# A fused attention and gMLP kernel: VectorE's exp as a squared square with a linear part summed by TensorE, denser Q projections, one accumulation for two output products, other head and tail

## The chip, the cores and the metric

The kernel runs on one core of one Trainium2 chip. The metric is the device time of one execution in microseconds (us), the median of several runs. Before the change it is 902.68 us, the median of 3 runs (899.88 to 902.83). The runs of the kernel before agree within a few tenths of a per cent; those of the kernels after the change scatter more, by about 1%. (A run is rated slow here when it is over 1.5% above the fastest run of its kernel.)

The engines are named as in the profile: PE is TensorE (matmuls), PEld its weight loads, ACT is ScalarE, DVE is VectorE, POOL is GpSimd, SP is the engine that issues most transfers.

## The reference

```python
# x: (1, 2048, 512); 32 heads of 16; one K and one V head for all (MQA); FH = 688
g = sigmoid((x * gate_w).sum(-1, keepdims=True))

q = (x @ wq).reshape(B, S, 32, 16).transpose(0, 2, 1, 3)
k, v = x @ wk, x @ wv
p = softmax(einsum("bhqd,bkd->bhqk", q, k) * 16 ** -0.5)
a = einsum("bhqk,bkd->bhqd", p, v).transpose(0, 2, 1, 3).reshape(B, S, 512) @ wo

z = gelu(x @ w_in)                       # (2048, 1376), tanh form
z1, z2 = z[..., :688], layernorm(z[..., 688:])
b = (z1 * (w_sp @ z2 + b_sp[:, None])) @ w_out

out = g * a + (1 - g) * b
```

The dominant work is the softmax: 32 x 2048 x 2048 exponentials. The product with `w_sp` (2048 x 2048, called the spatial matmuls below) is the largest dense product.

## The kernel before

The scores of four heads and 512 queries are made in blocks of 128 keys by 512 queries, 2048 blocks in all. A score matmul uses a 32-row tile of the array (a head has 16 rows, padded to 32), and up to four run together: in the trace of this kernel their starts lie 3 to 4 ns apart. The product with V (PV) uses a 32-column tile, again up to four together:

```python
def s_mm(dst_bank, blk, key):
    u, kt, g = blk
    mm(bank(dst_bank), KA[32*g:32*g+32, 128*kt:128*kt+128], QA[32*g:32*g+32, u % 4, :], True, True,
       [("K", kt // 4), ("Q", u % 4)], [key], tp=(32 * g, 0), chan="s", tag="S")     # 32 rows x 128 columns

def pv_mm(blk, src, key):
    ...
    mm(ps[32*g:32*g+32, 512*BO:512*BO+512], V1[:, kt, :], src, n == 0, n == NKT - 1,
       [("V", kt // 4), key], [("bk", BO)], tp=(0, 32 * g), chan="p", tag="PV")       # 128 rows x 32 columns
```

Most blocks get their exp on ACT, two or three blocks in one instruction from two alternating groups of PSUM banks. The others go to DVE in batches of four: one eviction per block, then nine operations over the batch (range reduction and a cubic polynomial):

```python
def d_A(m, i):
    op("dve", lambda v: v.tensor_scalar(DX[:, m % 2, 512*i:512*i+512], bank(BD), C_LOG2, 100.0, ALU.mult, ALU.min), ...)

def d_poly(m):
    return [
        (C4, ts(DN[:], x, BIG, BIG, ALU.add, ALU.subtract, ...)),
        (C2, tt(x, x, DN[:], ALU.subtract, ...)),
        (C4, ts(DT[:], x, E2[3], E2[2], ALU.mult, ALU.add, ...)),
        (C4, ts(n_i, DN[:], -126.0, 128.0, ALU.max, ALU.mult, ...)),
        (C2, tt(DT[:], DT[:], x, ALU.mult, ...)),
        (C4, ts(DT[:], DT[:], E2[1], None, ALU.add, ALU.bypass, ...)),
        (C2, tt(DT[:], DT[:], x, ALU.mult, ...)),
        (C4, ts(t_b, DT[:], E2[0], None, ALU.add, ALU.bypass, ...)),
        (C2, tt(pd.bitcast(I16), t_i, n_i, ALU.add, ...)),
    ]
```

All order is fixed when the program is built, by a small list scheduler in the source (`pe_pick`, `act_pick`, `dve_pick`). It plays the three engines forward with rough durations. Scores for ACT have the highest priority on PE. Everything that uses the whole array (projections, spatial matmuls, the products with `w_out` and `wo`) is cut into groups that share one PSUM bank, BM, and is slipped in where PE is free, one matmul at a time:

```python
elif misc["cur"].pos < len(misc["cur"].pieces):
    g = misc["cur"]                       # the group that owns bank BM

    def emit5():
        g.pieces[g.pos][1]()              # one full-array matmul
        g.pos += 1
    ...
    cands.append((now, 3, g.pieces[g.pos][0], emit5, fin5))
```

A group's bank comes free when DVE has evicted it, so each group ends with a wait for DVE. How many blocks go to DVE is decided by the same scheduler, as DVE has time (`new_batch`): 65 batches, 260 blocks; 1788 blocks are left for ACT in 715 instructions.

## Time and profile before

| | before |
|---|---|
| median time | 902.68 us |
| span of the profiled run | 897.0 us |
| ACT busy / DVE busy / PE busy | 94% / 94% / 89% |
| exp instructions on ACT | 715, 821.9 us |
| first exp starts, last exp ends | 12.6 us, 874.3 us |
| ACT idle between them | 16.8 us |
| mean granted TensorE clock | 0.978 |

First lines of the profile page of the kernel before: busy time of each engine, and busy tenths in 40 equal slices of the span (9 is 90% or more). PEclk is the granted TensorE clock in tenths of full speed.

```profile
PE 796.6 (89%) x5013; PEld 232.2 (26%) x5097; DVE 844.5 (94%) x1270; ACT 846.2 (94%) x729; POOL 7.0 (1%) x12
PE   5899989899995389999999999999999999999983
DVE  3299999999999999999999999999999999999995
ACT  4999999999999989999999999999999999999990
PEclk9999999999998599999999999999999999999998
```

ACT and DVE are both full from about 45 us to the end: the kernel is balanced between them. The clock row has one dip, in the stretch in which ACT does the gelu and PE has little to do (the clock is 0.50 from 284 to 315 us).

Costliest groups of instructions of the kernel before: line, engine, operation, output and input, shapes, count; busy us and mean ns of one; idle us of the engine just before them and what ended most of it.

```profile
L452 ACT ACTIVATE P<-ps 128x1536 bf16<-128x1536 f32 x715 | 821.9, 1258 | 24.6 <-PE ps L280 20.0
L280 PE MATMUL ps<-QA,KA 32*128 32x512 bf16 x2048 | 351.8, 387 | 52.5 <-DVE DX L466 28.0
L466 DVE TENSOR_SCALAR DX<-ps 128x512 f16<-128x512 f32 x260 | 177.3, 682 | 2.7 <-PE ps L280 2.4
L481 DVE TENSOR_TENSOR DT<-DT,DX 128x2048 f16<-128x2048 f16 x130 | 158.5, 1219 | 1.7
```

The exp costs 821.9/715 = 1.15 us of ACT each. A DVE operation over a batch costs 1.22 us as TENSOR_TENSOR and 0.685 us as TENSOR_SCALAR. DVE waited for nothing (2.7 us in all before its 260 evictions).

The windows view of the kernel before: from and to in us, length, then busy us and number of instructions of PE, PEld, DVE, ACT and POOL, the mean granted clock, the DMA share and GB/s.

```profile
core 0: us, PE busy (x) PEld busy (x) DVE busy (x) ACT busy (x) POOL busy (x), PEclk, DMA share, GB/s
740.00:840.00 100.00, 94.38 (x597) 27.46 (x605) 98.64 (x142) 98.88 (x87) 0.00 (x0) 1.00 0.00 1
...
783.00:809.00 26.00, 24.70 (x157) 7.31 (x159) 25.57 (x37) 25.78 (x24) 0.00 (x0) 1.00 0.00 1
```

The timeline of PE in the kernel before (start, length, what; matmuls of one kind that follow each other in one row):

```profile
785.80 0.38 PE L279 MATMUL ps<-wT,z 128*128 128x512 bf16 x1
786.11 0.39 PE L280 MATMUL ps<-QA,KA 32*128 32x512 bf16 x3
786.43 0.40 PE L280 MATMUL ps<-P,V 128*32 128x512 bf16 x3
...
788.48 0.39 PE L280 MATMUL ps<-QA,KA 32*128 32x512 bf16 x3
788.80 0.40 PE L280 MATMUL ps<-P,V 128*32 128x512 bf16 x3
```

A full matmul, three scores and three PVs follow each other at 0.32 us (786.11 to 786.43). The recorded lengths (0.38 to 0.40 us) are longer than that, so the matmuls overlap in the record; I go by the distance of the starts.

### The profile page before, as it was taken

What the parts mean: (1) busy time and instruction counts of PE and PEld (TensorE: products, weight loads), DVE (VectorE), ACT (ScalarE), POOL (GpSimd) and SP (SyncE); (2) the same over time, 40 slices, a digit from 0 to 9 for tenths busy, and PEclk for the clock granted to TensorE, in tenths of its full rate; (3) what the DMA queues carried; (4) which work ended last, traced back from release to release, by engine and by line L of the source; (5) the groups of instructions that cost most, each with busy time, mean ns of one, the idle gap of its engine ahead of it and who ended that gap; (6) DMA issues with size and microseconds to landing.
All of it is one profiled execution on the core that took longest, in us unless ns stands there. A gap on an engine that the chain in (4) does not pass through costs nothing.

```text
span 897.0 us, 13120 instructions
## 1 busy us (share of the span) xinstructions
PE 796.6 (89%) x5013; PEld 232.2 (26%) x5097; DVE 844.5 (94%) x1270; ACT 846.2 (94%) x729; POOL 7.0 (1%) x12
## 2 busy tenths in 40 slices
PE   5899989899995389999999999999999999999983
PEld 1323222222221022222222222222222222222220
DVE  3299999999999999999999999999999999999995
ACT  4999999999999989999999999999999999999990
POOL 1000000000000100000000000000000000000000
PEclk9999999999998599999999999999999999999998
DMA  6430000000000000001200003100002200000001
GB/s 131 130 72 1 1 1 1 1 1 1 1 1 1 0 1 1 1 1 33 63 1 1 1 1 60 35 1 1 1 1 48 48 1 1 1 1 1 17 31 49
DMA packets 48500, 16.66 MB, mean 19 GB/s; under 512 B 44161, under 2 KB 47921, under 8 KB 48434
## 3 DMA queue, kind: packets, MB, share of 16 engines
q1 hardware_dynamic: 45794, 15.23, 7.3%
q10 hardware_dynamic: 2640, 0.56, 0.4%
q8 instruction: 41, 0.67, 0.3%
q14 instruction: 25, 0.20, 0.1%
HBM read 3.20 MB, written 2.10 MB: 6 GB/s over the span
## 4 chain that ended last, share of the span: by engine, by line
DVE 69%; PE 18%; issue 8%; ACT 4%; DMA 1%; ACTq 0%; DVEq 0%
DVE DX L466 13%; DVE DT L481 13%; PE ps L280 12%; DVE DT L478 10%; DVE PD L481 7%; DVE DN L478 6%; DVE DX L481 6%; PE ps L279 6%; ACT P L452 3%; DVE bst L369 2%; DVE T L500 2%; DVE QA L324 2%; DVE z L348 1%; DVE z L355 1%; DVE z L402 1%
## 5 line engine op out<-in xcount | busy, mean ns | idle before, releaser
L452 ACT ACTIVATE P<-ps 128x1536 bf16<-128x1536 f32 x715 | 821.9, 1258 | 24.6 <-PE ps L280 20.0
L280 PE MATMUL ps<-QA,KA 32*128 32x512 bf16 x2048 | 351.8, 387 | 52.5 <-DVE DX L466 28.0
L280 PE MATMUL ps<-P,V 128*32 128x512 bf16 x1788 | 281.6, 392 | 1.9 <-DVE T L500 0.9
L466 DVE TENSOR_SCALAR DX<-ps 128x512 f16<-128x512 f32 x260 | 177.3, 682 | 2.7 <-PE ps L280 2.4
L280 PEld LDWEIGHTS ps<-QA,KA 32*128 32x128 bf16 x2048 | 85.6, 91 | 291.0 <-ACT P L452 141.6
L481 DVE TENSOR_TENSOR DT<-DT,DX 128x2048 f16<-128x2048 f16 x130 | 158.5, 1219 | 1.7
L280 PEld LDWEIGHTS ps<-P,V 128*32 128x32 bf16 x1788 | 68.2, 93 | 167.7 <-issue 158.9
L279 PE MATMUL ps<-wT,z 128*128 128x512 bf16 x349 | 108.2, 386 | 2.6 <-issue 2.2
L478 DVE TENSOR_SCALAR DT<-DT 128x2048 f16<-128x2048 f16 (+1 forms) x130 | 89.4, 688 | 2.4
L481 DVE TENSOR_TENSOR PD<-DT,DN 128x2048 int16<-128x2048 int16 x65 | 79.5, 1223 | 1.8
L481 DVE TENSOR_TENSOR DX<-DX,DN 128x2048 f16<-128x2048 f16 x65 | 79.4, 1221 | 1.5
L478 DVE TENSOR_SCALAR DT<-DX 128x2048 f16<-128x2048 f16 x65 | 44.5, 684 | 0.4
L478 DVE TENSOR_SCALAR DN<-DX 128x2048 f16<-128x2048 f16 x65 | 44.5, 684 | 0.3
L478 DVE TENSOR_SCALAR DN<-DN 128x2048 int16<-128x2048 f16 x65 | 44.5, 685 | 0.0
L279 PEld LDWEIGHTS ps<-wT,z 128*128 128x128 bf16 x384 | 28.9, 97 | 54.4 <-issue 45.5
L279 PE MATMUL ps<-xT,wq_pad 128*128 128x512 bf16 x111 | 36.3, 393 | 5.1 <-DVE z L348 1.8
L280 PE MATMUL ps<-PD,V 128*32 128x512 bf16 x260 | 31.9, 388 | 8.6 <-DVE PD L481 7.2
L279 PE MATMUL ps<-win,xT 128*128 128x344 bf16 x128 | 31.2, 315 | 1.3 <-DVE z L355 0.7
L279 PE MATMUL ps<-wout,z 128*128 128x512 bf16 x88 | 28.0, 385 | 2.3 <-DVE ybG L416 1.0
L279 PE MATMUL ps<-xT,win 128*128 128x512 bf16 x86 | 27.9, 385 | 2.2 <-DVE z L348 1.6
L279 PE MATMUL ps<-wo,OT 128*128 128x512 bf16 x59 | 18.9, 392 | 8.8 <-DVE outsb L432 3.7
L324 DVE CAST QA<-ps 128x512 bf16<-128x512 f32 x32 | 21.6, 676 | 2.7 <-PE ps L279 2.6
(66 smaller groups left out, 278.4 us busy)
## 6 DMA issues: line engine op xcount, KB each, us to landing
out_dram<-outsb SPq DMA_DIRECT2D x16, 128.0 KB, 1.7
win<-in_B_w_in_dram SPq DMA_DIRECT2D x1, 1376.0 KB, 6.5
wout<-in_B_w_out_dram SPq DMA_DIRECT2D x1, 640.0 KB, 4.4
wo<-in_A_wo_dram SPq DMA_DIRECT2D x8, 64.0 KB, 2.3
ybG<-in_A_wq_dram ACTq DMA_DIRECT2D x1, 448.0 KB, 4.7
wT<-in_B_w_sp_dram SPq DMA_TRANSPOSE x16, 4.4
xT<-in_A_x_dram SPq DMA_TRANSPOSE x4, 4.6
ybG<-in_A_wq_dram ACTq DMA_DIRECT2D x1, 64.0 KB, 3.8
```

The costliest lines, as they stand in the source:

```text
L279: return t.matmul(dst, lhsT, rhs, start=start, stop=stop)
L280: return t.matmul(dst, lhsT, rhs, start=start, stop=stop, tile_position=tp)
L324: ev = lambda: op("dve", lambda v: v.tensor_copy(QA[:, u % 4, :], bank(BM)), r=[BMK], w=[("Q", u % 4)], tag="Qev")
L348: ev = lambda: op("dve", lambda v: v.tensor_copy(z1[:, ft, 512 * tc:512 * tc + 512], bank(BM)), r=[BMK], w=[("z1", ft)], tag="z1ev")
L355: ev = lambda: op("dve", lambda v: v.tensor_copy(z2[:, FH * st + 344 * h:FH * st + 344 * h + 344], bank(BM, 344)), r=[BMK], w=[("z2", st)] ...
L369: dve_q.append((440, lambda st=st, h=h: op("dve", lambda v: v.bn_stats(bst[:, st, h, :], z2[:, FH * st + 344 * h:FH * st + 344 * h + 344]) ...
L402: ev = lambda: op("dve", lambda v: v.tensor_tensor(dst, ps[0:n, 512 * BM:512 * BM + 512], dst, ALU.mult), r=[BMK, ("z1", ft)], w=[("u", ft ...
L452: op("act", lambda a: a.activation(P[:, k % NP, 0:512 * n], ps[:, 512 * b0:512 * (b0 + n)], ACT.Exp), r=[("sc", k % 2)], w=[("P", k % NP)] ...
L466: op("dve", lambda v: v.tensor_scalar(DX[:, m % 2, 512 * i:512 * i + 512], bank(BD), C_LOG2, 100.0, ALU.mult, ALU.min), r=[("bk", BD)], w= ...
L478: return lambda: op("dve", lambda v: v.tensor_scalar(o, i, a, b, f, g), r=r, w=w, tag="dT")
L481: return lambda: op("dve", lambda v: v.tensor_tensor(o, i, j, f), r=r, w=w, tag="dTT")
L500: res = [(660, lambda: o("dve", lambda v: v.transpose(T1[:], bank(BO)), r=[("bk", BO)], w=["T1"], tag="T1"), setT(("O", u)))]
```

## The change

The intent is to make DVE's exp cheaper so that DVE can take blocks from ACT, and to shorten the head and the tail.

1. **Exp on DVE.** exp(x) is approximated by (u^2 + c)^2 with u linear in x, plus a linear function of x. The squared square takes three operations over a batch instead of nine. The linear part needs no elementwise work: summed over keys against V it is a product of Q with a small matrix (K^T V, precomputed), so TensorE adds it to the PV accumulation by two extra 32-column matmuls per head group ("corrections", 256 in all).
2. **Dense Q.** Q is projected for 128 columns at a time instead of 64 padded ones, so half the Q matmuls and evictions go. A copy of K shifted by 16 rows serves the odd heads.
3. **yb and wo in one PSUM group.** The products with `w_out` and `wo` accumulate in one bank, with the gate ratio folded into the softmax's normalisation, so the intermediate `ybG` and its eviction go.
4. **Head and tail.** Warm-up matmuls at the start, other order of transfers and projections; the last four output tiles are accumulated in free banks before the last exp.

The core of the diff (cuts marked by `...`):

```diff
         def d_A(m, i):
-            op("dve", lambda v: v.tensor_scalar(DX[:, m % 2, 512*i:512*i+512], bank(BD), C_LOG2, 100.0, ALU.mult, ALU.min), ...)
+            op("dve", lambda v: v.tensor_scalar(X[:, m % NX, 512*i:512*i+512], bank(BD), PA, PB, ALU.mult, ALU.add), ...)
         def d_poly(m):
-            return [ ... nine operations ... ]
+            return [
+                (C2, lambda: op("dve", lambda v: v.tensor_tensor(x, x, x, ALU.mult), ...)),
+                (C4, lambda: op("dve", lambda v: v.tensor_scalar(x, x, PC, None, ALU.add), ...)),
+                (C2, lambda: op("dve", lambda v: v.tensor_tensor(PD[:, m % ND, :], x, x, ALU.mult), ...)),
+            ]
+        def cor_mm(u, g, z):
+            n = (64 - units[u]["hi"]) // 4
+            if z == 0:
+                pv_raw(u, g, MC[:, n-1, 2*g + u % 2, :], QA[:, (u // 2) % NQ, :], ["MC", ("Q", (u // 2) % NQ)], "COR")
+            else:
+                pv_raw(u, g, CC[:, n-1, :], ones[:], ["CC", "ones"], "COR")
...
-        def g_yb(t2): ...
-        def g_wo(t2): ...
+        def g_fin(t2):
+            ...
+            return Group("fin", [(C512, lambda ft=ft: yb_mm(t2, ft, BM)) for ft in range(6)] +
+                                [(C512, lambda jp=jp: wo_mm(t2, jp, BM)) for jp in range(4)], [(680, ev)], ...)
...
-        first = deque([g_K(0), g_Q(0), g_V(0), g_K(1), g_V(1), g_K(2), g_V(2), g_K(3), g_V(3), g_Q(1)])
+        first = deque([g_V(0), g_K(1), g_K(2), g_V(1), g_K(3), g_V(2), g_V(3), g_MC(), g_R(0), g_Q(1), g_R(1), g_R(2), g_R(3)])
```

## The prediction

> **What bounds it now.** The table of engine busy time gives ACT 846 and DVE 845 of 897 us. By windows, 440 to 840 us has both 98 to 99% busy: balanced. PE shows 95% there, but the timeline says that is not its peak: a stream of full matmuls advances every 0.216 us, and each change between full, row-tiled (scores) and column-tiled (PV) matmuls advances 0.32 us, about 0.107 us for the change. [...] The first exp starts at 12.6 us (the first matmuls advance only every 0.43 us), and the last ends at 874.3, leaving a tail of 22.7 us: serial wo groups and DVE evictions.

> **Changes, costed** (counts from the built program):
> - VectorE exp: nine ops of 128x2048 per batch of four blocks (five TENSOR_SCALAR at 0.685, four TENSOR_TENSOR at 1.22) become three (two at 1.22, one at 0.685). With four evictions at 0.68 a batch falls from 11.0 to 5.85 us. [...]
> - The schedule takes only 89 batches, up from 65. Blocks on ACT fall from 1788 to 1692, ACT exps from 715 to 677. At 821.9/715 = 1.15 us each that is -44 us of ACT.
> - DVE: 89x5.85 = 521 instead of 717 for exp; the rest about 180 instead of 197 (16 fewer Q evictions at 0.68, no ybG at 0.74; new squares). Less the records' overlap, about 645 us busy, 77%: DVE becomes slack.
> - PE: 64 Q matmuls fewer, 256 correction matmuls (64 waves) more. In the built order waves (matmuls on different tiles, run together) fall from 2585 to 2472, mode changes from 2086 to 1946: at 0.216 and 0.107 us, 782 to 742 us. Not the bound.
> - Head: warm-up matmuls, Q projected without waiting for K's eviction and evicted by ACT: first exp about 9.5 us, -3.
> - Tail: yb and wo of the last four tiles are accumulated beforehand in free banks; after the last exp remain PV, transposes, four matmuls, evictions on two engines, output: about 12 us, -10.

> **Critical path.** ACT alone then sets the pace. Sum: 9.5 + 677x1.15 + about 26 (gelu, table loads, small) + about 15 idle (now 17) + 12.5 = 841 us of span; the runs are 5.7 us over the span: **about 846 us**, 80% range **830 to 862**, that is -6%. Of the gain of 57, 44 is ACT blocks moved; most of DVE's saving (200 us) is not spent.

> Chances: faster 0.95, same 0.04, slower 0.01.

> **What would show it.** Right: ACT 97% or more of the time from first to last exp, about 805 us busy; DVE 74 to 80%; squared-square ops at 1.22 and 0.69; first exp near 9.5; tail 11 to 14 us. Wrong: ACT idle grown beyond 25 us with waits on PE (then PE order or its waits on DVE bound it); DVE still over 90% (ops slower than counted); first exp later than 11.

> **What would make it wrong.** PE being the true limit in the stretch after gelu, where all spatial and output groups lie; correction matmuls holding up the PV order; the shifted K copy by DMA arriving late for odd heads; the head's matmuls staying at half pace; or the check flag tripping the slow path.

## The result and the profile after

The kernel after takes **873.42 us**, the median of 4 runs (871.48 to 881.95), against 902.4 us of the kernel before, the median of 4 runs. A ratio in this document is the mean time of one kernel's runs over that of the other's of the same rounds, so it is not quite the ratio of the medians quoted. (It also leaves out the profiled run of the kernel that is measured.) Here it is 0.9707 (95% interval 0.9659 to 0.9755): the change is worth 3%, half of what was predicted, and the time lies 11 us above the range.

| | before | predicted | after |
|---|---|---|---|
| median time, us | 902.4 | 846 | 873.4 |
| batches on DVE / exps on ACT | 65 / 715 | 89 / 677 | 89 / 677 |
| DVE busy, us | 844.5 | 645 | 665.8 |
| ACT busy, us | 846.2 | 805 | 810.5 |
| first exp starts, us | 12.6 | 9.5 | 9.9 |
| from last exp to the end, us | 22.6 | 12.5 | 15.0 |
| ACT idle between first and last exp, us | 16.8 | 15 | **37.8** |
| mean granted clock | 0.978 | (not considered) | **0.920** |

First lines of the page of the kernel after, to be held against those of before:

```profile
PE 798.3 (92%) x5270; PEld 228.7 (26%) x5347; DVE 665.8 (77%) x1014; ACT 810.5 (93%) x698; POOL 10.9 (1%) x17
PE   8989999999990999999999999999989999999996
DVE  3678888788989876877887888878668777867662
ACT  6889999999999789999999999999999999999893
PEclk9789999999995599999999999999979999995757
```

DVE has become slack, as intended. The clock row has new dips: at the start, in slice 30, and in the last four slices, beside that of the gelu.

The groups of the kernel after that answer to those shown of before:

```profile
L539 ACT ACTIVATE P<-ps 128x1536 bf16<-128x1536 f32 (+1 forms) x677 | 784.2, 1245 | 37.9 <-PE ps L276 32.7
L276 PE MATMUL ps<-QA,KA 32*128 32x512 bf16 x2048 | 327.3, 408 | 43.4 <-DVE X L563 23.5
L563 DVE TENSOR_SCALAR X<-ps 128x512 f16<-128x512 f32 x356 | 243.8, 685 | 131.6 <-PE ps L276 131.3
L570 DVE TENSOR_TENSOR X<-X 128x2048 f16<-128x2048 f16 x89 | 108.9, 1223 | 2.6
L571 DVE TENSOR_SCALAR X<-X 128x2048 f16<-128x2048 f16 x89 | 61.0, 685 | 0.6
```

The new DVE operations cost exactly what the old ones did per operation (1.223 and 0.685 us). The idle time before the exps grew from 24.6 to 37.9 us (this view also counts the wait before the first exp, so it is not the table's number), and 32.7 of it ended by a PE matmul. DVE now waits 131.3 us for PE. So both elementwise engines wait for PE, while PE's busy time hardly changed (796.6 and 798.3 us). The chain that ended last, by engine, before and after, says the same; first the line of before:

```profile
DVE 69%; PE 18%; issue 8%; ACT 4%; DMA 1%; ACTq 0%; DVEq 0%
```

and that of after:

```profile
PE 64%; DVE 25%; issue 6%; ACT 4%; ACTq 0%
```

The windows view of the kernel after (columns as before):

```profile
440.00:540.00 100.00, 96.71 (x668) 28.24 (x678) 79.74 (x113) 98.08 (x86) 0.00 (x0) 1.00 0.12 26
740.00:840.00 100.00, 94.31 (x573) 23.59 (x578) 74.76 (x109) 93.49 (x82) 0.00 (x0) 0.78 0.00 1
...
781.00:782.00 1.00, 0.93 (x7) 0.19 (x4) 1.00 (x2) 1.00 (x1) 0.00 (x0) 1.00 0.00 0
782.00:783.00 1.00, 0.68 (x7) 0.25 (x7) 0.96 (x3) 1.00 (x3) 0.00 (x0) 0.50 0.00 0
...
783.00:809.00 26.00, 25.03 (x129) 4.98 (x127) 20.23 (x27) 23.38 (x21) 0.00 (x0) 0.50 0.01 1
```

In the middle (440 to 540) ACT is as full as before. In 740 to 840 it is not: 93.5 us instead of 98.9. The clock falls at 782.0 us from 1.00 to 0.50 and stays there until 812.7 us. In 783 to 809 PE is busy 96% of the time at half the clock and does 129 recorded matmuls where the kernel before did 157; ACT does 21 exps instead of 24. The timeline of PE there:

```profile
786.03 0.60 PE L276 MATMUL ps<-QA,KA 32*128 32x512 bf16 x2
786.57 0.61 PE L276 MATMUL ps<-P,V 128*32 128x512 bf16 x2
787.12 0.61 PE L276 MATMUL ps<-QA,KA 32*128 32x512 bf16 x4
787.66 0.61 PE L276 MATMUL ps<-P,V 128*32 128x512 bf16 x3
```

Now scores and PVs advance every 0.54 us instead of 0.32. And there are hardly any full matmuls between them: the spatial groups were done earlier, the last of their matmuls starts at 773 us (814 before), and most of what is left waits for the last heads.

The half-clock stretches, from the clock records of the traces (not a line of the page; worked out from them), in us: before, 284 to 315 (the gelu) and nothing else until the last exp; after, 20.8 to 24.2, 31.1 to 41.3, 44.7 to 51.5, 263 to 308 (the gelu), 638.6 to 648.9 (the spatial groups wait for the next transfer of `w_sp`), 782.0 to 812.7, 823.0 to 829.8, 833.2 to 857.1. That is 134.5 us between first and last exp, against 30.7 us before. 21.7 of the 37.8 us of ACT idle time fall into these stretches, against 2.9 of 16.8. The records have one gap: those of the kernel before begin at 18.05 us. Until then its scores and PVs advance by 0.54 us, from there on by 0.32, so its first exps too ran at half clock, about 5 us that the clock row and the 0.978 do not show. (The records of the kernel after begin at 7.2 us, before its first exp.)

The clock records of both traces show two values only, 1.00 and 0.50, and the edges lie on a grid of 3.41 us: in the kernel before the stretch at half clock is 9.00 times 3.413 us long and those at full clock beside it 78.00 and 168.00 times; in the kernel after the fall at 782 us lasts 9.00 times as long. In the stretches after 638 us PE is busy 96 to 100% of the time (in that of the gelu, half of it: 22.9 of 44.3 us). The clock does not go with PE's busy time: in the 3.4 us before the fall at 782 us PE was busy for 2.7 us, and the clock then stayed at half for 30.7 us of which PE was busy 29.4. What it goes with was the question for the experiments.

### The profile page after: what moved, and what is told of

It reads as the page before. It is cut to its first block, busy times and chain, and to the rows that moved or that the text cites. A ratio compares the mean times of both kernels' runs of the same rounds, so it can differ in the third digit from the quotient of the medians.

```text
span 870.0 us, 13369 instructions
## 1 busy us (share of the span) xinstructions
PE 798.3 (92%) x5270; PEld 228.7 (26%) x5347; DVE 665.8 (77%) x1014; ACT 810.5 (93%) x698; POOL 10.9 (1%) x17
## 4 chain that ended last, share of the span: by engine, by line
PE 64%; DVE 25%; issue 6%; ACT 4%; ACTq 0%
PE ps L276 44%; PE ps L275 20%; DVE X L563 6%; DVE X L570 4%; ACT P L539 4%; DVE PD L572 3%; DVE bst L467 2%; DVE X L571 2%; DVE T L582 1%; DVE z L453 1%; DVE Tn L586 1%; DVE QA L341 1%; DVE z L477 1%; DVE OT L590 1%; DVE z L446 0%
## 5 line engine op out<-in xcount | busy, mean ns | idle before, releaser
L539 ACT ACTIVATE P<-ps 128x1536 bf16<-128x1536 f32 (+1 forms) x677 | 784.2, 1245 | 37.9 <-PE ps L276 32.7
L276 PE MATMUL ps<-QA,KA 32*128 32x512 bf16 x2048 | 327.3, 408 | 43.4 <-DVE X L563 23.5
L563 DVE TENSOR_SCALAR X<-ps 128x512 f16<-128x512 f32 x356 | 243.8, 685 | 131.6 <-PE ps L276 131.3
L570 DVE TENSOR_TENSOR X<-X 128x2048 f16<-128x2048 f16 x89 | 108.9, 1223 | 2.6
L572 DVE TENSOR_TENSOR PD<-X 128x2048 bf16<-128x2048 f16 x89 | 108.7, 1221 | 1.9
L571 DVE TENSOR_SCALAR X<-X 128x2048 f16<-128x2048 f16 x89 | 61.0, 685 | 0.6
L582 DVE STREAM_TRANSPOSE T<-ps 128x512 f32<-128x512 f32 x32 | 22.7, 711 | 16.9 <-PE ps L276 16.9
L276 PE MATMUL ps<-QA,MC 128*32 128x512 bf16 x128 | 20.0, 428 | 0.5 <-DVE ct L422 0.5
L276 PE MATMUL ps<-ones,CC 128*32 128x512 bf16 x128 | 19.8, 427 | 0.0
L275 PE MATMUL ps<-xT,wq 128*128 128x512 bf16 x55 | 17.9, 385 | 1.1 <-DVE z L453 0.6
```

Source lines behind the costliest of these rows:

```text
L275: return t.matmul(dst, lhsT, rhs, start=start, stop=stop)
L276: return t.matmul(dst, lhsT, rhs, start=start, stop=stop, tile_position=tp)
L539: op("act", lambda a: a.activation(P[:, k % NP, 0:512 * n], ps[:, 512 * b0:512 * (b0 + n)], ACT.Exp), r=[("sc", k % 2)], w=[("P", k % NP)] ...
L563: op("dve", lambda v: v.tensor_scalar(X[:, m % NX, 512 * i:512 * i + 512], bank(BD), PA, PB, ALU.mult, ALU.add), r=[("bk", BD)], w=[("X", ...
L570: (C2, lambda: op("dve", lambda v: v.tensor_tensor(x, x, x, ALU.mult), r=[k], w=[k], tag="dU")),
L571: (C4, lambda: op("dve", lambda v: v.tensor_scalar(x, x, PC, None, ALU.add), r=[k], w=[k], tag="dV")),
```

## The experiments

The first theory, a guess from the trace of the kernel after (called A), was: **the clock is granted by the share of the array that is in use, each matmul weighted by its rows times its columns, in windows of 3.41 us; below about 0.31 it is halved; tiled matmuls alone cannot get it back; the fall costs ACT its feed.** The rivals: too much work lowers the clock (B); it is busy time that counts, with any matmul alike; it is not the clock but the amount or the order of PE's work in this stage; it is the corrections that hold up the PV order. 15 kernels were run besides the kernel after; 13 of them were timed against the kernel before on the same chip, two only stream matmuls and were run once.

All times are medians of a kernel's runs. The traces are of one run each, the first of its series, which in eight of the thirteen timed kernels is the slowest; idle and half-clock times read from a trace belong to that run and not to the median.

### 1. `fill`: a full matmul where the array would be left to tiles

After the gelu, whenever bank BM is free and the planned use of the array in the last 3.41 us is under 0.40, the scheduler issues one full matmul on data that nobody reads. There are 52 of them.

```diff
+        def array_use(now):                    # planned use, each matmul weighted by its area
+            while use and use[0][0] < now - 3413.0:
+                use.popleft()
+            return sum(w_ for _, w_ in use) / 3413.0
+        def filler():
+            mm(bank(BM), xT[:, 0, 0:128], xT[:, 0, 0:512], True, True, [("x", 0)], [BMK], tag="fill")
...
+            if (now > 320000.0 and misc["cur"] is None and misc["free"] + LAT <= now and tl_state[12] == 0
+                    and st_["ua"] < NU and array_use(now) < 0.4):
+                cands.append((now, 5, C512 + 60, filler, None))
...
                 if t2 == 12:
-                    ok = misc["free"] + LAT <= now
+                    ok = misc["free"] + LAT <= now and (st_["ua"] >= NU or st_["ua"] == NU - 1 and units[NU-1]["hi"] - units[NU-1]["lo"] <= 30)
```

> The changed kernel plus 52 filler matmuls of 128x128 by 512 (useless, into the idle misc bank), placed after the gelu stage wherever the planned use of the array over 3.4 us falls under 0.40; a matmul on a quarter of the array is counted as a quarter. Theory A (the half clock comes from too little use of the array, counted by area, in fixed windows of 3.41 us, under about 0.31): no half clock between 310 us and the last exp, ACT idle after 310 us falls from about 20 to under 8 us, 855 to 861 us in place of 873. Rival B (too much work or current lowers the clock): at least as much half clock as now, time not under 871. Rival C (the order of PE and its waits starve ACT whatever the clock): time within 4 us of 873 or longer.

Measured: 861.32 us, ratio 0.9551 (0.9501 to 0.9602), 12 us faster than the kernel after although it does 52 matmuls more and nothing less. Half clock between first and last exp fell from 134.5 to 64.1 us, with only one short stretch left after the gelu (839.1 to 845.9). (The change of `t2 == 12`, which lets a tail group start later, is in `fill_tile` too, so it is not what makes the difference to that run.) The time is 0.3 us over the upper edge of what was expected. The window that was at half clock in the kernel after:

```profile
783.00:809.00 26.00, 23.96 (x168) 6.71 (x167) 20.98 (x29) 25.93 (x24) 0.00 (x0) 1.00 0.00 1
```

The clock is 1.00, ACT is full again, and PE is busy for less time with more matmuls. That useless work makes the kernel faster is hard to explain by anything but the clock.

### 2. `fill_tile`: the same slots, but a 32-row tile

```diff
-            mm(bank(BM), xT[:, 0, 0:128], xT[:, 0, 0:512], True, True, [("x", 0)], [BMK], tag="fill")
+            mm(bank(BM), xT[0:32, 0, 0:128], xT[0:32, 0, 0:512], True, True, [("x", 0)], [BMK], tp=(0, 0), tag="fill")
```

> The same 52 fillers in the same places, but on 32 of the 128 rows (32x128 by 512): the same PE time, a quarter of the array. Theory A (use counted by area): half clock about as in the changed kernel (640 to 650 us, most of 782 to 855), time 869 to 878. Rival D (the clock follows PE's busy time or its gaps, whatever part of the array works): as the full fillers, no half clock after 310 us, 855 to 861 us.

Measured: 887.37 us over four runs, two of them rated slow (889.45 and 893.63); the fast ones are 874.46 and 885.3. The ratio, 0.9856 (0.9809 to 0.9903), has the two slow runs in it; the two fast runs alone give 0.975. So it is no faster than the kernel after (0.9707), and that it is slower is not shown. 869 to 878 had been expected. The profiled run, the fastest, has half clock for 110.6 us between first and last exp:

```profile
642.00:658.00 16.00, 16.00 (x76) 3.01 (x74) 8.33 (x10) 12.30 (x12) 0.00 (x0) 0.50 0.41 84
783.00:809.00 26.00, 24.18 (x176) 6.77 (x173) 21.59 (x32) 26.00 (x24) 0.00 (x0) 1.00 0.01 1
820.00:832.00 12.00, 12.00 (x65) 2.43 (x58) 6.41 (x8) 9.17 (x8) 0.00 (x0) 0.50 0.00 1
```

In the first and the last of these windows PE is busy for 100% of the time and the clock is 0.50: so the clock does not go with busy time. The middle row is a miss: there the clock was expected at half and is full, from 782 to 819 us, with tiles alone. The fillers take the same slots in the issue order as in experiment 1, and they too add to the array's use. Counted by active rows, as experiment 8 will, the windows from 782 to 816 us had 0.38 to 0.50; by area, several of them had only 0.30 to 0.33. So this control is weaker than it was meant to be: it took the clock away in part of the stage, not in all of it.

### 3. `pace`: no matmul added, the full ones spread

A spatial or output matmul is issued only while the planned use is at most 0.52; otherwise it is put off.

```diff
-            elif misc["cur"].pos < len(misc["cur"].pieces):
+            elif misc["cur"].pos < len(misc["cur"].pieces) and not (now > 300000.0 and misc["cur"].name in ("sp", "fin") and array_use(now) > 0.52):
```

> No filler: the same matmuls as the changed kernel, but after the gelu stage a spatial or output matmul is issued only while the planned use of the array over the last 3.4 us is at most 0.52, so that this work lasts to the end rather than running out 75 us before it. Theory A: no half clock from 310 us to the last exp but for at most two windows, 855 to 864 us. Rival C (order alone; slower progress of the spatial work can only hurt): 873 or longer.

Measured: 856.36 us, ratio 0.9512 (0.9469 to 0.9555), 17 us faster than the kernel after with exactly its mathematics (88 batches instead of 89). After the gelu the clock is full until the last exp. PE's busy time is 789.7 us (798.3 in the kernel after), so it is hardly the amount of work that helps, but when it is done.

```profile
783.00:809.00 26.00, 25.14 (x179) 7.18 (x178) 21.21 (x32) 25.79 (x24) 0.00 (x0) 1.00 0.01 1
```

### 4. `nocor`: the corrections left out

```diff
-                    pvt[(u, g)] = 16 + (2 if n else 0)
-                units[u]["cor"] = 8 if n else 0
+                    pvt[(u, g)] = 16
+                units[u]["cor"] = 0
```

> The 256 correction matmuls taken out (wrong result on purpose: the linear part of the exp is missing). Rival E (the corrections hold up the PV order and cost ACT its pace): at least 12 us faster than 873. Theory A: a matmul on a quarter of the array less lowers the use further, half clock in the same stretches, time between 862 and 876, thus at most a third of the miss of 27 us.

Measured: 876.13 us, ratio 0.9732 (0.9689 to 0.9775), like the kernel after. (862 to 876 was expected.) Half clock in 638.7 to 655.8, 775 to 809 and 816 to 857 us. The corrections are not the cause. Its four runs, one and the same program, show besides that time goes with the clock where no order differs: 869.85, 875.89, 876.37 and 882.57 us at mean granted clocks of 0.917, 0.907, 0.906 and 0.896. The result was wrong on purpose and still passed the comparison, so that comparison would not notice a missing linear part.

### 5. `fill_all`, `fill_all_d`, `fill_all_2`: fillers from the start; DVE's own score first; fewer batches

`fill_all` has fillers from 9 us on (90 in all), also one ahead of a score group in the head. `fill_all_d` lets DVE evict its own score block before anything else (92 batches). `fill_all_2` allows at most two batches per head group (62 batches, 720 exps on ACT), which takes away most of the change's main effect.

```diff
# fill_all, against fill
+                    extra = 12000.0 < now < 60000.0 and array_use(now) < 0.38
...
+                        if extra:
+                            mm(bank(EB[k % 2][0]), xT[:, 0, 0:128], xT[:, 0, 0:512], True, True, [("x", 0)], [("sc", k % 2)], tag="fill")
...
-            if (now > 320000.0 and misc["cur"] is None ...
+            if (now > 9000.0 and misc["cur"] is None ...
# fill_all_d, against fill_all
-                cands.append((dbank["ready"], 3, 600, e1, f1))
+                cands.append((dbank["ready"], -1, 600, e1, f1))
# fill_all_2, against fill_all
-                if un["hi"] - un["lo"] < (RMIN if u < NU - 1 else RLAST) + DB or un["hi"] <= 64 - 4 * NMAX:
+                if un["hi"] - un["lo"] < (RMIN if u < NU - 1 else RLAST) + DB or un["hi"] <= 64 - 4 * 2:
```

> Fillers from the start: 90 in all, in the head (some into the score banks just before the scores overwrite them), through the gelu stage and after it; 88 batches on VectorE. Theory A (use of the array by area sets the clock): no half clock between the head and the last exp, ACT idle before 100 us from 8.3 to 3 to 5 us, from 100 to 320 us from 11.3 to 5 to 8, time 846 to 853 (the fillers after gelu alone: 861). Rival (the losses in head and gelu stage come from waits for loads and for VectorE, not from the clock): 856 or more.

> As fill_all, and VectorE evicts a score block of its own before any other work, so that the schedule comes to 92 batches. If ACT sets the pace once the clock is kept up, 16 blocks fewer at 0.46 us each take off 7 us: 839 to 847. If PE or the PV order sets the pace: no faster than fill_all.

> As fill_all, but at most two batches of a head on VectorE: 62 batches in place of 88, so 104 more blocks on ACT. If ACT sets the pace and a block is worth 0.46 us of it: 48 us longer than fill_all (44 to 53). If PE sets the pace: less than 25 us longer, since PE's work falls a little.

Measured: `fill_all` 861.86 us, ratio 0.9536. **This was a miss**: the fillers did not keep the clock up in the head. The half-clock stretches there became 13.7 to 27.4 and 34.2 to 54.7 us, longer than in the kernel after, and ACT's idle time before 100 us did not fall (9.4 us; 8.3 in the kernel after):

```profile
35.00:54.00 19.00, 19.00 (x104) 4.83 (x102) 8.59 (x21) 15.12 (x15) 1.47 (x3) 0.50 0.20 39
```

PE is busy for the whole of it, with fillers, at half clock. The time lies where the rival of the text on record had it (856 or more); but as the clock was not kept up, the run does not decide between them. Experiments 8 to 10 tell why the clock fell.

`fill_all_d`: 852.56 us, ratio 0.9427, outside the expected 839 to 847 for the same reason, but 9.3 us under `fill_all` (7 expected).

`fill_all_2`: 903.63 us, ratio 1.0002 (0.9965 to 1.0039), 41.8 us slower than `fill_all` (44 to 53 expected). This is the plainest result about the change itself: with the cheap exp, the dense Q, the new head and tail, but without more blocks on DVE, **nothing is gained** on balance. The change's net gain is that of the blocks taken from ACT, about 0.40 us each: (88 - 62) x 4 = 104 blocks more on ACT, 41.8/104 = 0.40 (`fill_all` has 88 batches, 679 exps). In the profiled run the head and the tail are still shorter than in the kernel before, by 1.8 and 7.8 us, but ACT's idle time is 12.7 us longer (29.5 against 16.8) and there are five exps more. The clock is not ruled out as a part of this: in spite of 177 fillers instead of 90, that run has 86.6 us of half clock, `fill_all`'s 64.7.

### 6. `before_fill`: fillers in the kernel before

```diff
+            if now > 9000.0 and misc["cur"] is None and misc["free"] + LAT <= now and st_["ua"] < NU and array_use(now) < 0.4:
+                cands.append((now, 5, C512 + 60, filler, None))
```

> The kernel before with the same rule of fillers (47, nearly all in the gelu stage). Theory A: there the half clock of 31 us goes, but ACT and VectorE are both full and most of it lay under gelu, so 894 to 901, within 1% of before; the gain of the fillers belongs to the changed kernel. If fillers help by something else than the clock (say, they keep the queue or the weights busy): a gain like the 12 us that they gave the changed kernel or more.

Measured: 904.87 us, ratio 1.0011 (0.9972 to 1.0049), with 47 fillers. The small gain expected (894 to 901 us) did not come, and within 1% it is the kernel before. But the fillers did not do what they were put there for: in the profiled run 20.5 us of half clock stayed at the gelu (295.7 to 299.1 and 305.9 to 323.0), and 13.7 us came up in the head (22.6 to 36.2), where there are no fillers, so that there were 34.1 us of it instead of 30.7. So useless matmuls as such made nothing faster here; what a full clock at the gelu would be worth to the kernel before it does not show.

### 7. `pace_d`, `pace_d_gelu`, `fill_d`: the better versions

`pace_d` is `pace` with a limit of 0.57 and DVE's own score first (92 batches). `pace_d_gelu` adds 53 fillers around the gelu. `fill_d` is `fill_all_d` with fillers only from 240 us on, where the planned use falls under 0.42 instead of 0.40 (96 batches, 71 fillers).

```diff
# pace_d, against pace
-            ... and array_use(now) > 0.52):
+            ... and array_use(now) > 0.57):
-                cands.append((dbank["ready"], 3, 600, e1, f1))
+                cands.append((dbank["ready"], -1, 600, e1, f1))
```

> The paced kernel (no filler; limit 0.57 in place of 0.52) with VectorE evicting a score block of its own before any other work: 92 batches. If ACT sets the pace when the clock is kept up, 3 to 4 batches more than the paced kernel's 88 take off 6 to 7 us: 847 to 853 against 856. If PE or the PV order sets it: 855 or more. No half clock between 330 us and the last exp, but for a window or two.

> As pace_d with 53 fillers through the gelu stage. If the half clock there (44 us, 12 of them after the work resumes) costs ACT its pace: 4 to 8 us faster than pace_d, ACT idle from 100 to 320 us under 6 us in place of 11. If the fillers only come in the way of the scores: no faster, or slower.

> No pacing; fillers from the gelu stage on wherever the planned use falls under 0.42 (71), and VectorE's eviction first: 96 batches. By theory A with ACT as the bound: within 5 us of pace_d_gelu, 840 to 850.

Measured: `pace_d` 851.46 us (ratio 0.9418), `pace_d_gelu` 849.42 us (0.9410, 0.9378 to 0.9441), `fill_d` 849.76 us (0.9399, 0.9351 to 0.9447). They cannot be told apart. All beat the kernel before by 6% and the kernel after by about 23 us. The gelu fillers were expected to bring 4 to 8 us; the 2 us seen are within the noise, and ACT's idle time from 100 to 320 us was 7.6 us instead of 6.2, so nothing is shown for them.

### 8. `clock`: what the clock goes with

Theory A had explained `fill` and `pace`; against it stood the head of the `fill_all` kernels and the full clock of `fill_tile` from 782 to 819 us. This kernel computes nothing of the reference; it streams matmuls of 512 columns in stretches, each of one kind.

```python
full(96)                     # 128 rows x 128 columns, back to back
rows(1, 80)                  # one 32-row tile at a time
full(64); rows(2, 80)        # two 32-row tiles together
rows(1, 80); rows(2, 60)     # the same pair, started at half clock
rows(3, 60)                  # three together
full(64); col(80)            # one 32-column tile at a time (128 rows)
full(64)                     # then one full and n = 2, 3, 4, 5, 6, 8, 10 row tiles, repeated
...                          # then full matmuls with waits for ACT
```

> A kernel of another kind: it computes nothing of the reference (its output is zero, on purpose), it only streams matmuls of 512 columns back to back on TensorE, in stretches of about 17 us or more, so that the clock record can be read for each mixture by itself. One 32-row tile is a quarter of the array. Theory A (the clock is granted by the share of the array in use, in a fixed window of 3.41 us, lost below about 0.31, regained above about 0.33, counted in full-clock time): full matmuls stay at 1.00; one 32-row tile at a time (0.25) falls to 0.50, though TensorE is never idle; two row tiles at a time (0.5) after full matmuls stay at 1.00, but the very same stream started at half clock (0.25 of what full clock could do) stays at 0.50; three row tiles at half clock (0.375) return to 1.00; one 32-column tile falls like a row tile; in the series of one full matmul and n row tiles (n = 2, 3, 4, 5, 6, 8, 10; estimated use 0.376, 0.351, 0.334, 0.322, 0.314, 0.302, 0.293) the clock falls somewhere from n = 5 to n = 10 and not before; full matmuls with waits for ScalarE between them fall only where their own share is under about 0.31. Rival D (the clock goes by how busy the engine is, any matmul counting alike): 1.00 in every stretch except perhaps those that wait for ScalarE. Rival M (tiled matmuls, or changes to and from full ones, lower the clock as such): two row tiles fall as one does, and the series with n = 2, which has most changes per us, falls first.

Measured (one run, 528.95 us), in the windows view; the stretches are one row tile, a pair after full matmuls, a pair started at half clock, three together, and one column tile:

```profile
38.00:53.00 15.00, 15.00 (x36) 5.11 (x35) 0.00 (x0) 0.00 (x0) 0.00 (x0) 0.50 0.00 0
75.00:88.00 13.00, 13.00 (x124) 5.84 (x122) 0.00 (x0) 0.00 (x0) 0.00 (x0) 1.00 0.01 1
123.00:145.00 22.00, 22.00 (x106) 7.50 (x102) 0.00 (x0) 0.00 (x0) 0.00 (x0) 0.50 0.00 1
153.00:163.00 10.00, 10.00 (x138) 4.43 (x134) 0.00 (x0) 0.00 (x0) 0.00 (x0) 1.00 0.01 2
181.00:193.00 12.00, 12.00 (x57) 5.41 (x56) 0.00 (x0) 0.00 (x0) 0.00 (x0) 1.00 0.00 0
```

PE is busy for 100% of every one of them. Rows two and three are the same stream of pairs, at full clock and at half, by history alone: at half clock the pair does half as many matmuls (106 recorded in 22 us, against 124 in 13 us; by the count below 0.25 of the rows in use against 0.49), and the clock did not come back within the stretch. That is the trap. Busy time and tiling as such are out: 100% busy goes with 0.50 and with 1.00, and so do pairs of row tiles.

The last row contradicts theory A. One 32-column tile at a time is also a quarter of the array, and the clock stayed full for 17 us (1.00 in the row shown, where the row tile of the same area has 0.50). It does not go with the area. In the mixed series the clock fell already at n = 3, at an estimated use of 0.35, not from n = 5 on, so the threshold of 0.31 was wrong as well.

I then recomputed the use of every 3.41 us window of all 14 traces (3425 windows) from the matmul records and the clock records, under several weightings, and asked which one tells whether the next window has the full clock. A matmul of 512 columns of data counts 0.213 us in full-clock time, half of the 0.427 us from one to the next at half clock (in the kernel before from 6.7 to 7.6 us; the first row above has 36 in 15 us); one of fewer columns counts in proportion, an assumption of this count. Tiles that start together are taken together.

| weighting | best threshold | windows that disagree, of 3425 |
|---|---|---|
| rows times columns (theory A) | 0.33 | 51 |
| **active rows / 128, tiles together at most 1** | **0.375** | **18** |

In the second weighting a wave of m scores counts m/4 of its time, and a wave of PVs counts in full, however many tiles it has. This is a fit to the same data (421 of the windows are followed by half clock), so it needed a test of its own. These figures stand in no view; they are worked out from the records. A second count with a program of its own gave nearly the same: 52 and 19 windows, of 3411, at the same two thresholds. In the traces of the kernels before and after alone, a third count, with each matmul placed at its recorded start, has 14 and 6 windows of 505 that disagree; placed 0.15 us later, it has 12 for each, so these two traces alone do not tell the weightings apart, and the streams of this experiment and the next must. All this describes the records of these runs; how the clock is decided they do not show.

### 9. `clock2`: the refitted rule on mixtures that had not been used

Stretches of matmuls with K = 64, 56, 52, 48, 44 and 40 active rows; a column tile started at half clock; full-height matmuls of 64, 32 and 8 columns; bursts of full matmuls within row tiles.

> Streams of matmuls only, output zero on purpose. The refitted rule: the clock counts the share of array rows in use (a matmul counts by its active rows over 128, whatever its columns; tiles that run together add up to at most 1), per 3.41 us window in full-clock time, and is full from 0.375 on. With matmuls of K active rows back to back the use is about 0.99 K/128, so K = 64 (0.49), 56 (0.43), 52 (0.40) stay at 1.00, K = 44 (0.34) and 40 (0.31) fall to 0.50, and K = 48 (0.37) is on the edge, rather falling. One 32-column tile at a time, started at half clock (0.49), brings the clock back. Full-height matmuls of 64, 32 or 8 columns stay at 1.00. A burst of eight full matmuls within a stream of 32-row tiles at half clock brings the clock back for one to three windows; nine repeats of one full and one row tile at half clock (0.37 to 0.40) are near the edge. Full matmuls with a wait for ScalarE after each stay at 1.00 where their share of the time is over 0.375. Rival by area: 64, 32 and 8 columns fall for the last two (0.25 and 0.06), and the column tile at half clock (0.12) stays at half. Rival by blocks of 32 rows (a matmul counts by whole row groups): K = 40 to 64 all count as 0.5 and stay at 1.00.

Measured (one run, 445.32 us), in the windows view; the rows are K = 64, K = 52, K = 48, the column tile after its start at half clock, full height with 8 columns, and one 32-row tile:

```profile
29.00:40.00 11.00, 11.00 (x53) 4.79 (x52) 0.00 (x0) 0.00 (x0) 0.00 (x0) 1.00 0.00 0
80.00:92.00 12.00, 12.00 (x58) 5.18 (x57) 0.00 (x0) 0.00 (x0) 0.00 (x0) 1.00 0.00 0
113.00:129.00 16.00, 16.00 (x39) 5.49 (x38) 0.00 (x0) 0.00 (x0) 0.00 (x0) 0.50 0.00 0
246.00:254.00 8.00, 8.00 (x39) 3.59 (x38) 0.00 (x0) 0.00 (x0) 0.00 (x0) 1.00 0.00 0
308.00:318.00 10.00, 10.00 (x48) 4.00 (x46) 0.00 (x0) 0.00 (x0) 0.00 (x0) 1.00 0.00 0
335.00:347.00 12.00, 12.00 (x30) 4.14 (x29) 0.00 (x0) 0.00 (x0) 0.00 (x0) 0.50 0.00 0
```

### 10. `pace_d_burst`, `pace_d_burst2`: is the head slow by the clock alone?

By the refitted rule `fill_all`'s failure in the head has a reason: single fillers between tiles at half clock gave windows of 0.32 to 0.37, just under 0.375. A run of full matmuls should do. `pace_d_burst2` adds four bursts of eight to `pace_d`; `pace_d_burst` adds three bursts of ten, and single fillers between them.

```diff
+        bursts = deque([13000.0, 22000.0, 31000.0, 42000.0])
...
+                    nf = 8 if bursts and now > bursts[0] else ... else 0
                     def emit():
                         T["now"] = now
+                        if nf > 1:
+                            bursts.popleft()
+                        for _ in range(nf):
+                            mm(bank(EB[k % 2][0]), xT[:, 0, 0:128], xT[:, 0, 0:512], True, True, [("x", 0)], [("sc", k % 2)], tag="fill")
                         for i_, blk in enumerate(bl):
```

> pace_d with three bursts of ten full matmuls ahead of score groups in the head (planned near 13, 26 and 40 us) and single fillers between them while the planned use is under 0.45, to 60 us; 94 batches instead of 92, so about 3 us less on ScalarE. If the head was slow by the clock alone, a burst puts one window over 0.375 and the clock comes back; half clock before 100 us shrinks from pace_d's 49 us to under 25, ScalarE idle before 100 us from 19.1 to 8 to 12 us, and the time is 838 to 848 us (pace_d: 851.46, ratio 0.9418). If the head is slow for other reasons (late data, or PE too full with fillers), idle stays at 15 us or more and the time at 850 or more.

> pace_d with four bursts of eight full matmuls in the head (planned near 13, 22, 31 and 42 us) and no single fillers; 95 batches, so about 5 us less on ScalarE than pace_d. The clock comes back at each burst, but may fall again where only tiles and a few projections run between bursts: half clock before 100 us 15 to 40 us, ScalarE idle before 100 us 10 to 15 us, time 840 to 850 us. If pace_d_burst holds full clock and this one does not, what keeps the clock in the head is a steady share of full matmuls; if neither does, the rule is wrong for the head.

Measured: `pace_d_burst2` 849.5 us (848.07 to 853.61), ratio 0.9393 (0.9341 to 0.9445): as fast as the other good versions, not faster beyond the noise. `pace_d_burst` 860.64 us over all five runs, ratio 0.952 (0.9465 to 0.9574), where 838 to 848 had been expected; one run, the profiled one, is rated slow (871.66), and the median of the other four is 859.6. The clock did what the rule says, but for one window: in both, the half-clock windows with a burst had 0.365 to 0.50 of the rows in use (the 0.365, just under the edge, is one of the 2 that disagree) and were followed by full clock, and half clock before 100 us shrank from `pace_d`'s 47.8 us to 13.6 us in `pace_d_burst` and 20.5 us in `pace_d_burst2`. But ACT's idle time before 100 us fell only from 19.1 to 13.6 and 13.0 us, less than hoped for. That ACT is not fed while a burst runs is the likely reason; it was not tested. So the clock is a part of the head's loss and can be bought back, at a price that leaves little. What the rest of the head needs stays open. Why `pace_d_burst` is 8 us slower than `pace_d` is also open; its profile is of the slow run, so I don't use it for that, and its two figures above are of that run.

## Why the prediction was right or wrong

**Right: the mechanism of the change.** The DVE operations cost 1.223 and 0.685 us for the same 128 x 2048 elements, 89 batches were made, ACT's exps fell from 715 to 677. DVE became slack at 77%, as predicted, at 666 us instead of 645. `fill_all_2` shows that without the blocks moved off ACT nothing is gained on balance. The first exp starts at 9.9 us (9.5).

**Wrong: "PE ... Not the bound", and with it "about 15 idle (now 17)".** This is the step that failed. It priced PE with durations at full clock (0.216 us per wave and 0.107 us per change between kinds) and took it for granted that these hold whatever else is changed. In these runs they held while about 0.375 or more of the array's rows were in use (20 of 4051 windows disagree); below it a wave with its change took 0.54 us instead of 0.32. The sum of the prediction, term by term:

| term | predicted, us | measured, us |
|---|---|---|
| first exp starts | 9.5 | 9.9 |
| 677 exps | 778.6 (at 1.15) | 784.2 (at 1.158) |
| **ACT idle between first and last exp** | **15** | **37.8** |
| gelu, table loads, small | 26 | 23.2 (what is left to the last exp's end at 855.1) |
| tail | 12.5 | 15.0 |
| span | 841 | 870.0 |

The idle term alone is 23 of the 29 us by which the span was missed. (The time was missed by 27: the profiled run is 1.8 us over its span, not 5.7.) The exps' term belongs to it in part: their records overlap less in the kernel after (0.087 us an exp against 0.109 before: the mean of one less the busy time over the count), and `pace` had its 679 exps busy for 779.9 us. The prediction named the sign: "ACT idle grown beyond 25 us with waits on PE". Among its risks stood "PE being the true limit in the stretch after gelu" and "the head's matmuls staying at half pace"; both came, by a cause that it did not name. It had even measured matmuls at 0.43 us in the head of the kernel before, and did not ask when they would return to that.

**How the change brought it about.** Computed from the trace by the refitted rule, scores and PVs alone use 0.33 of the rows in the kernel before (740 to 840 us) and 0.36 after (440 to 540 us): in both kernels the attention alone lies below or about at the threshold, and it is the full matmuls between them, 0.22 before, that carry the clock. In the kernel before, the full groups stretch out to 890 us, and from 320 us to the last exp the use never fell below 0.405. In the kernel after they run ahead, wait for `w_sp` once, and end early.

What lets them run ahead is not shown. My first reading was that DVE, now slack, evicts bank BM sooner. The traces do not bear it out: after 320 us an eviction starts on average 0.51 us after the last full matmul in the kernel before and 0.49 us in the kernel after. What differs is that there are 79 such evictions before and 48 after (denser Q, one group instead of two for the output products), that the first spatial matmul starts at 294 us instead of 313, and that the full matmuls of one spatial group take 11.5 us on average instead of 13.0. No run took these apart.

| stretch | full-clock share of rows in use | of which tiles | clock |
|---|---|---|---|
| before, 783 to 812 us | 0.557 | 0.346 | 1.00 |
| after, 740 to 778 us | 0.585 | 0.380 | 1.00 |
| after, 783 to 812 us | 0.324 | 0.308 | 0.50 |
| `pace`, 783 to 812 us | 0.607 | 0.371 | 1.00 |
| `fill`, 783 to 812 us | 0.529 | 0.376 | 1.00 |

In the kernel after the windows just before the falls after the gelu had 0.352, 0.313, 0.300 and 0.330; the lowest window at full clock that was followed by full clock again had 0.404. Once at half clock, a wave of scores and one of PVs take 0.54 us each instead of 0.32 (against 0.427 and 0.216 us for matmuls of one kind, so the change between kinds is about 0.11 us at either clock), and alternating they can use at most about 0.213 x (0.75 + 1) / 1.08 = 0.345, an estimate from the 0.54 and 0.427 us with three scores in a wave; the windows that stayed at half clock measured 0.24 to 0.41, nearly all under 0.375. So scores and PVs in turn did not get the clock back here. Tiles in another mixture did: at 648.9 and 829.8 us the clock returned after windows of tiles alone (0.386 and 0.378 by the second count), in which PVs and corrections, each wave counting in full, followed each other. These shares are computed from records of which a few per cent are missing, so the second decimal is about what they are worth.

**A consequence for reading the numbers.** By the busy table PE was 92% busy in the kernel after and 89% before, and it was never the bound by its own count of waves. Busy time did not tell here how much PE got done: from 783 to 809 us PE was 95% busy at full clock in the kernel before and 96% busy at half clock in the kernel after, with 157 and 129 recorded matmuls.

**What remains.** With the clock held after the gelu (`pace`) 17 of the 27 us between prediction and result came back, at 856.4 us. The rest lies mainly in the head and around the gelu: `pace` has 7.2 us of ACT idle before 100 us and 11.4 from 100 to 320 us, against 2.1 and 6.0 in the kernel before. In experiment 10 the head's share was not to be had by bursts of full matmuls; what else it needs, and what the gelu stage needs, is open.

## What to carry to other kernels

When a change makes background work run ahead, ask what that work did where it was; here the full matmuls, spread over the whole run, carried TensorE's clock. Read the granted clock stage by stage before pricing a matmul, and in a stage of row-tiled matmuls count the share of array rows in use per 3.41 us: below 0.375 (the edge of these runs) the matmuls cost up to 1.7 times as much here (0.54 against 0.32 us), and scores and PVs in turn did not climb back. Spreading the full matmuls added no work and was worth 17 us; dummy ones were worth 12 us in the kernel after, and nothing in the kernel before.
